# Seven key tiles of a softmax denominator added up on GpSimd and VectorE in float32, with one float32 product in place of seven bf16 ones

## The chip, the cores and the metric

The kernel runs on one core of one Trainium2 chip. The metric is the device time of one execution in microseconds (us). An execution's time is a little longer than the span of its profile.

## The reference

Eight batches of attention with twelve heads, 448 positions and head size 64, on normalised queries and keys, and then a two-layer network on the 3584 x 768 result. Cut to what matters:

```python
q_n = q / (np.linalg.norm(q, axis=-1, keepdims=True) + 1e-06)
k_n = k / (np.linalg.norm(k, axis=-1, keepdims=True) + 1e-06)
scores = np.matmul(q_n, k_n.transpose(0, 1, 3, 2)) / tau
attn = np.exp(scores - np.max(scores, axis=-1, keepdims=True))
attn = attn / (np.sum(attn, axis=-1, keepdims=True) + 1e-09)
x = np.matmul(attn, v)          # heads side by side: (3584, 768)
h = x @ w_in                    # (768, 2048)
out = np.maximum(0.01 * h, h) @ w_out
```

The change is about `np.sum(attn, ...)`, the denominators of the softmax.

## The kernel before

Scores are bounded because queries and keys are normalised, so the kernel takes no maximum. It works with transposed scores: keys lie on the partitions and queries along the free dimension. ScalarE writes exp(scores) as bf16 tiles "pe" of 128 partitions x 896 (line 423). The denominators are then sums over partitions and over seven tiles, which the kernel gets as a product on TensorE with ones (PE in the profile), accumulated in PSUM.

The whole program is in an order written out by hand: each engine carries out its own instructions in the order of the code. Two batches of head pairs go through an older layout (lines 653 to 861). From the third batch on there are 18 *units* of two head pairs each and ten *groups* of one or two units (lines 186 to 191). A unit has seven key tiles (126 in all), and the loop at line 896 goes through them three at a time, in 42 *visits*. A visit does the following.

- `normalise(s)` (line 250): VectorE sums the two parts of the norm, takes the reciprocal, and multiplies queries or keys by it (line 260) into `qn`. `s` is a half of a unit, its queries or its keys; which visit prepares which half is worked out at lines 879 to 882: no half in visits 9, 16, 23, 30 and from 37 on.
- `prepare()` (line 901): VectorE transposes `qn`, and SyncE's DMAs bring it into place; SyncE loads raw data for a later half; GpSimd copies one element of `qn` ("hold", line 619), which makes it wait for VectorE, and then squares the raw data of the half after the next (line 216); VectorE sums the squares of the next half (line 232).
- `quad_tiles` (line 406): PE computes score tiles with eight small matmuls each, ScalarE takes the exponential.
- `group_products(g, e)` (line 427): in the visit after a group's last tile PE makes the denominators (`e` is None: 56 matmuls of pe with ones), in the next one or two visits the products with the values (`e` 0 and 1: 56 matmuls with `vq`). They stand behind the visit's first score tile. `group_logs` and `group_inverse` make 1/denominator on ScalarE by Ln and Exp, and `group_scale` multiplies on VectorE (line 467) into `xT`.
- pieces of the two-layer network of earlier batches (`first`, line 485, and `second`, line 523), dealt out so that PE always has work (lines 930 to 942). `second` ends with a VectorE copy (line 538) into `osb` and a DMA to the output.
- `roots(s + 1)` on ScalarE, before the last of those pieces.

The denominators with ones stand in visits 3, 7, 12, 15, 19, 24, 28, 33 and 38, and for the last group behind visit 41.

The very last `second` copies its 384 columns in two halves, one on VectorE and one on ScalarE, and sends them off with one DMA. In the first microseconds, `load_main` and `load_rem` bring the first pairs in with DMAs from SyncE (SP) and ScalarE's queue (ACT).

Of the kernel before, what the change touches and what calls it, by code (L numbers as in the profile page):

```python
# [8 lines left out]
F32 = mybir.dt.float32  # L9
BF16 = mybir.dt.bfloat16  # L10
AF = mybir.ActivationFunctionType
ALU = mybir.AluOpType
# [4 lines left out]
def kernel(  # L17
# [10 lines left out]
    nc = tc.nc  # L28
    B, H, S, D = q.shape
# [13 lines left out]
    WARM = 20  # L43
    NEWQ = 2 * NQ
    PER = 3
    assert REM == 64 and D == 64

    ctx.enter_context(tc.manual_schedule())
# [4 lines left out]
    qnp = ctx.enter_context(tc.tile_pool(name="qn", bufs=3))  # L53
    ttp = ctx.enter_context(tc.tile_pool(name="tt", bufs=2))
    qtp = ctx.enter_context(tc.tile_pool(name="qt", bufs=6))
    pep = ctx.enter_context(tc.tile_pool(name="pe", bufs=25))
    vqp = ctx.enter_context(tc.tile_pool(name="vq", bufs=2))
    rbp = ctx.enter_context(tc.tile_pool(name="rb", bufs=2))
    xtp = ctx.enter_context(tc.tile_pool(name="xt", bufs=2))
    htp = ctx.enter_context(tc.tile_pool(name="ht", bufs=1))  # L60
    osp = ctx.enter_context(tc.tile_pool(name="os", bufs=3))
# [4 lines left out]
    gp = nc.gpsimd  # L66
# [8 lines left out]
    def banks(count, keep=None):  # L75
        lo, hi = (0, 8) if not deals["apart"] else (0, 4) if count == 2 else (4, 8)
        x = min(
            (i for i in range(lo, hi, count) if not set(range(i, i + count)) & set(kept.values())),
            key=lambda i: max(age[i : i + count]),
        )  # L80
        deals["n"] += 1
        age[x : x + count] = [deals["n"]] * count
        if keep:
            kept[keep] = x
        return ps[:, x] if count == 1 else ps[:, x : x + count]
# [41 lines left out]
    def load_rem(pairs, engs=(nc.sync, nc.sync)):  # L127
        lo, hi = 2 * (pairs[0] % 3), 2 * (pairs[-1] % 3) + 2
        part = early[pairs[0] // 3][:, lo:hi, 3]
        for i, (x, eng) in enumerate(zip((q, k), engs)):  # L130
            eng.dma_start(  # L131
                out=part[64 * i : 64 * i + 64],
                in_=x[0, 2 * pairs[0] : 2 * pairs[-1] + 2, MAIN:S].rearrange("h p d -> p h d"),
            )
# [238 lines left out]
    def totals(j):  # L373
        sm = banks(1)
        strip_products(j, sm, lambda g, ki: ones, lambda g: ones_rem[:, g // 2])
        rb = rbp.tile([128, 2, S], F32, name="rb")[:, 0]
        nc.scalar.activation(rb, sm[:, :S], func=AF.Ln)
        nc.scalar.activation(rb, rb, func=AF.Exp, scale=-1.0)
        rbs[j] = rb
# [21 lines left out]
        if (j, e) in kept:  # L401
            given_back((j, e))

    pq = {}

    def quad_tiles(which):

# [19 lines left out]
    def group_products(g, e):  # L427


        us = [u for u, (gg, _) in enumerate(UNITS) if gg == g]  # L430
        two = len(us) == 2
        po = banks(2)
        for i in range(7):
            for strip in range(4):
                for w in range(2):
                    x, a = strip // 2, strip % 2
                    rows = slice(64 * w, 64 * w + 64)
                    weights = ones[rows] if e is None else (
                        vq[g][rows, strip if two else a, i]
                        .rearrange("p (d e) -> p e d", e=2)[:, e if two else w ^ x]  # L440
                    )
                    nc.tensor.matmul(  # L442
                        out=po[32 * strip : 32 * strip + 32, w, :S],
                        lhsT=weights, rhs=pq[us[x if two else 0], i][rows, a, :],
                        start=(i == 0), stop=(i == 6),
                    )
        return po

    def group_logs(g, po):
        grb[g] = rbp.tile([128, 2, S], F32, name="rb")  # L450
        nc.scalar.activation(grb[g], po[:, :, :S], func=AF.Ln)

    def group_inverse(g):
# [68 lines left out]

    def second(c, ts, half):
        c0, n = chunk_cols(c)
        po2 = banks(1)
        for m in range(MT):
            nc.tensor.matmul(  # L527
                out=po2[:, :HALF],
                lhsT=hT[c][:, m, ts * 128 : (ts + 1) * 128],
                rhs=w_out_sb[:, m, half * HALF : (half + 1) * HALF],  # L530
                start=(m == 0), stop=(m == MT - 1),
            )
        if half == 0:
            osb[c, ts] = osp.tile([128, D_model], F32, name="osb")
        o = osb[c, ts]
        last = c == B - 1 and ts == n // 128 - 1
        cut = HALF // 2 if last and half == 1 else HALF
        nc.vector.tensor_copy(out=o[:, half * HALF : half * HALF + cut], in_=po2[:, :cut])  # L538
        if cut < HALF:
            nc.scalar.copy(out=o[:, half * HALF + cut : (half + 1) * HALF], in_=po2[:, cut:HALF])  # L540
        if half == 1 or last:
            h0 = half * HALF if last else 0
            x, end, row = c0 + ts * 128, c0 + (ts + 1) * 128, 0
            while x < end:
                dst, cnt = rows_of(c, x, end)
                eng = nc.scalar if cut < HALF and row else nc.sync
                eng.dma_start(
                    out=dst[:, h0 : (half + 1) * HALF],
                    in_=o[row : row + cnt, h0 : (half + 1) * HALF],
                )  # L550
                x += cnt
                row += cnt


    work = {}
# [14 lines left out]
    load_main(0, (nc.sync, nc.scalar))  # L570
    load_rem((0,), (nc.sync, nc.scalar))
    load_main(1)
    load_rem((1, 2))
    load_main(2)
    load_main(3)
    load_rem((3, 4, 5))
# [14 lines left out]
    nc.vector.memset(warm, 1.0)  # L591
    ones = cpool.tile([128, 32], BF16, name="ones")
    nc.vector.memset(ones, 1.0)
    ones_rem = cpool.tile([128, 2, 32], BF16, name="ones_rem")
    nc.vector.memset(ones_rem, 0.0)
    for i in range(2):
# [58 lines left out]
    for s in range(NPAIR):  # L655
        j = s // 2 - 1 if s >= 2 else None
        even = s % 2 == 0
        n = s + 2 if 0 < s < NPAIR - 2 else None
        last = s == NPAIR - 1
        if not last:  # L660
            scores(s, (0,))
        if s in (1, 2):
            roots(s + 1)
        scores(s, (1,))
        if j is not None and not even:
            products(j, 1)
        if j is not None and even:
            totals(j)
        elif not last:
            fill(2)  # L670
        if n:
            sums(n, (0,))
        if not last:
            normalise(s + 1)
        if s == 0:
            load_qk(7)
        elif s in (2, 3):
            hold_loads(s + 1)
            load_qk(s + 6)
        if s == 3:  # L680
            sums(n, (1,))
        if late:
            scale(late.pop(), 1)
        if j is not None and not even:
            scale(j, 0)
        if last:
            scale(j, 1)
            sums(NPAIR)
            sums(NPAIR + 1)
            load_w_out(0)  # L690
        else:
            hold(qn[s + 1][:, 6, 0, 0:1])
        squares(s + 3)
        if s == 0:
            load_v_rem(0, range(2, 4))
        if s in (1, 2):
            load_v(s)
        if last:
            load_v(NQ)
            load_v_rem(1)  # L700
        elif s < 2:
            load_w_in(s)
        elif s > 2:
            load_w_in(s - 1)
        if n and even:
            sums(n, (1,))
        scores(s, (2,))
        if last:
            for m in range(2):
                first(0, m, (0, 2))  # L710
            scores(s, (3,))
            for kt in (1, 3):
                for m in range(2):
                    first(0, m, (kt,))
        elif not even:
            fill(2)
            if s == 3:
                roots(n)
                transposes(s + 1)
            scores(s, (3,))  # L720
            if s == 1:
                transposes(s + 1)
                sums(n, (1,))
            fill(2)
        elif s == 0:
            fill(2)
            transposes(1)
            sums(2)
            fill(2)
        else:  # L730
            transposes(s + 1)
            products(j, 0)
            if s == NPAIR - 2:
                scores(s + 1, (0,))
            if n:
                roots(n)
        if j is not None and not even and not last:
            late.append(j)
# [61 lines left out]
    load_v(s // 2 + 2)  # L800
    hold_loads(s + 4)
    load_qk(s + 7)
    squares(s + 6)
    feed_groups(0, 1)

    def settle(s):  # L810
        normalise(s)
        if s >= OLD:
            transposes(s)
        hold(qn[s][:, 6, 0, 0:1])
        squares(s + 2)

    scores(s + 2, (0, 1, 2))
    feed_groups(0, 1)
# [3 lines left out]
    roots(s + 5)  # L822

    scores(s + 3, (0, 1, 2))
    settle(s + 5)
    hold_loads(s + 5)
    load_qk(s + 8)
    feed_groups(0, 1)
# [62 lines left out]
        for n in range(len(visits))  # L891
    ]

    held = []
    fed = 0
    for n, tiles in enumerate(visits):
# [22 lines left out]
        if scaling:  # L919
            prepare()  # L920
        quad_tiles(tiles[1:])
        if g is not None and e is None:
            group_inverse(g)
        for u, i in tiles:
# [15 lines left out]
            now.append(held.pop(0)[1][1])  # L940
            done += w
        fed += done
        for fn in now[:-1]:
            fn()
        roots(s + 1)
        for fn in now[-1:]:
            fn()
    g = len(GROUPS) - 1
    group_logs(g, group_products(g, None))
# [46 lines left out]
```

## Time and profile before

| what | value |
|---|---|
| runs of before | 417.6, 418.37 (median) and 528.36 us |
| the profiled execution | 418.31 us |
| its span | 416.5 us |
| granted TensorE clock | 0.999 |
| the 560 matmuls with ones | 15.1 us busy |
| GpSimd's squares of a half, 36 | 60.9 us busy |

"Busy" is the time in which an engine has an instruction under way; matmuls overlap, so the chain of work that ended last tells better what one of them costs. In the timeline a row is the start, the duration, the engine, the line of the code, the operation, output <- input, shapes and types, and, in brackets, how long the engine had been idle before and what released it. POOL is GpSimd, DVE VectorE, ACT ScalarE, SP SyncE.

### The profile page before, as it was taken

How to read it: one execution, taken by the hardware profiler on the slowest of the kernel's cores; microseconds unless marked ns; L12 is line 12 of the kernel's file. 1: busy time of each engine (PE TensorE's matmuls, PEld its weight loads, DVE VectorE, ACT ScalarE, POOL GpSimd, SP SyncE). 2: the span in 40 equal slices, each digit the busy share in tenths (PEclk: the TensorE clock that was granted, in tenths of full speed). 3: DMA queues.
4: the chain of work that ended last, by engine and by line, in shares of the span. 5: the costliest groups of instructions: out<-in, count | busy, mean ns of one | idle time of the engine just before them, and what ended most of it. 6: DMA issues, size and time to landing. Idle time of an engine off the chain costs nothing.

```text
span 416.5 us, 11298 instructions
## 1 busy us (share of the span) xinstructions
PE 406.0 (97%) x4769; PEld 211.1 (51%) x4785; DVE 221.4 (53%) x386; ACT 250.7 (60%) x432; POOL 114.2 (27%) x149
## 2 busy tenths in 40 slices
PE   8799999999999999999999999999999999999996
PEld 3235555544455555544455555554445555654563
DVE  6778776856678555766484964464621301210021
ACT  4897877288657785667865688547674464014300
POOL 4887343433234132413331433122210000000000
PEclk9999999999999999999999999999999999999999
DMA  7999998684377841884285681742442100020022
GB/s 185 248 219 216 210 234 183 160 237 120 59 209 189 208 115 32 210 229 95 51 190 154 149 232 45 174 126 83 91 90 77 41 39 3 38 77 0 2 76 76
DMA packets 41820, 53.82 MB, mean 129 GB/s; under 512 B 12458, under 2 KB 32170, under 8 KB 41770
## 3 DMA queue, kind: packets, MB, share of 16 engines
q1 hardware_dynamic: 25866, 41.07, 35.1%
q0 software_dynamic: 15488, 11.80, 19.7%
q8 instruction: 37, 0.61, 0.6%
q10 hardware_dynamic: 416, 0.23, 0.2%
q14 instruction: 13, 0.11, 0.1%
HBM read 45.61 MB, written 11.01 MB: 136 GB/s over the span
## 4 chain that ended last, share of the span: by engine, by line
PE 92%; ACT 3%; DVE 2%; DMA 1%; SPq 1%; issue 1%; ACTq 0%; DVEq 0%
PE ps L494 35%; PE ps L527 35%; PE ps L442 9%; PE ps L417 7%; PE ps L366 3%; PE ps L346 2%; ACT pe L355 2%; DVE qn L270 1%; DMA xT<-in_k_dram 1%; PE ps L284 1%; SPq L131 0%; SPq L139 0%; DVE qkT L325 0%; PE ps L608 0%; ACT norms L246 0%
## 5 line engine op out<-in xcount | busy, mean ns | idle before, releaser
L527 PE MATMUL ps<-w_out_sb,hT 128*128 128x384 bf16 x896 | 151.3, 326 | 0.0
L494 PE MATMUL ps<-xT,w_in_sb 128*128 128x384 bf16 (+1 forms) x754 | 150.1, 352 | 0.8 <-issue 0.2
L423 ACT ACTIVATE pe<-ps 128x896 bf16<-128x896 f32 x126 | 108.9, 916 | 46.0 <-PE ps L417 46.0
L527 PEld LDWEIGHTS <-hT 128*128 128x128 bf16 x896 | 85.4, 98 | 64.9 <-issue 10.3
L494 PEld LDWEIGHTS <-w_in_sb 128*128 128x128 bf16 x768 | 72.7, 98 | 74.1 <-issue 9.7
L505 ACT ACTIVATE hT<-ps 128x384 bf16<-128x384 f32 (+1 forms) x128 | 67.5, 553 | 56.0 <-PE ps L494 54.9
L538 DVE COPY osb<-ps 128x384 f32<-128x384 f32 (+1 forms) x56 | 30.9, 551 | 100.4 <-PE ps L527 100.4
L216 POOL TENSOR_TENSOR sq<-qk_h 128x896 f32<-128x896 f32 x36 | 60.9, 1691 | 9.3 <-DMA qk_h<-in_k_dram 6.7
L619 POOL CAST seen<-qn 128x1 f32<-128x1 bf16 x46 | 8.5, 185 | 177.1 <-DVE qn L260 162.5
L260 DVE TENSOR_TENSOR qn<-qk_h,r 128x896 bf16<-128x896 f32 x36 | 43.0, 1195 | 1.2
L355 ACT ACTIVATE pe<-ps 128x896 bf16<-128x896 f32 x42 | 36.1, 917 | 3.3 <-PE ps L346 3.3
L232 DVE TENSOR_REDUCE ss<-sq 128x14 f32<-128x910 f32 x36 | 37.9, 1052 | 0.0
L417 PE MATMUL ps<-qkT 64*32 64x448 bf16 x1008 | 36.5, 353 | 0.0
L253 DVE TENSOR_REDUCE r<-norms 128x14 f32<-128x28 f32 x48 | 8.6, 179 | 49.4 <-ACT norms L246 48.8
L467 DVE TENSOR_TENSOR xT<-ps,rb 128x448 bf16<-128x448 f32 x32 | 18.4, 617 | 23.2 <-PE ps L442 21.5
L306 DVE STREAM_TRANSPOSE tt<-qn 128x448 f32<-128x448 f32 x36 | 29.6, 822 | 0.9
L442 PE MATMUL ps<-pe,vq 64*32 64x448 bf16 x1008 | 27.0, 349 | 0.0
L245 ACT ACTIVATE ss<-ss 128x14 f32<-128x14 f32 x48 | 10.3, 215 | 24.8 <-DVE ss L232 24.0
L417 PEld LDWEIGHTS <-qkT 64*32 64x32 bf16 x1008 | 13.1, 91 | 19.3 <-issue 14.5
L442 PEld LDWEIGHTS <-vq 64*32 64x32 bf16 x1008 | 14.5, 92 | 8.0 <-issue 0.3
L442 PE MATMUL ps<-pe,ones 64*32 64x448 bf16 x560 | 15.1, 349 | 0.0
L346 PE MATMUL ps<-qkT 64*64 64x448 bf16 (+1 forms) x132 | 12.6, 359 | 2.2 <-ACT pe L355 1.3
(54 smaller groups left out, 218.3 us busy)
## 6 DMA issues: line engine op xcount, KB each, us to landing
qk_h<-in_q_dram SPq DMA_DIRECT2D x36, 224.0 KB, 4.0
qk_h<-in_k_dram SPq DMA_DIRECT2D x36, 224.0 KB, 4.6
out_dram<-osb SPq DMA_DIRECT2D x20, 384.0 KB, 2.3
qkT<-tt SPq DMA_DIRECT2D x72, 56.0 KB, 3.3
qkT<-tt SPq DMA_DIRECT2D x36, 112.0 KB, 3.4
vq<-in_v_dram POOLq DMA_DIRECT2D x16, 224.0 KB, 4.9
w_in_sb<-in_moe_w_in_dram POOLq DMA_DIRECT2D x4, 768.0 KB, 10.0
w_out_sb<-in_moe_w_out_dram POOLq DMA_DIRECT2D x2, 1536.0 KB, 21.4
```

The costliest lines, as they stand in the source:

```text
L216: gp.tensor_tensor(sq[:, :, :D], x, x, op=ALU.mult)
L232: nc.vector.tensor_reduce(ss[s], sqs[s], axis=AX.X, op=ALU.add)
L260: nc.vector.tensor_tensor(qn[s].rearrange("p m d e -> p m e d"), raw[s].rearrange(f"p ({t[1:-1]} d) -> p m e d", e=n, d=D), r.rearrange(f" ...
L306: nc.vector.transpose(out=to.rearrange(("p g (c m) -> p m g c", "p g (m c) -> p m g c")[which], m=7), in_=qn[s].bitcast(F32).rearrange("p ...
L355: nc.scalar.activation(out=dst, in_=sc[:, :, :S], func=AF.Exp, scale=inv_tau)
L417: nc.tensor.matmul(out=sc[32 * strip : 32 * strip + 32, a, :S], lhsT=x[rows, c0 : c0 + 32], rhs=x[rows, 0:S], start=True, stop=True,)
L423: nc.scalar.activation(out=pq[u, i], in_=sc[:, :, :S], func=AF.Exp, scale=inv_tau)
L442: nc.tensor.matmul(out=po[32 * strip : 32 * strip + 32, w, :S], lhsT=weights, rhs=pq[us[x if two else 0], i][rows, a, :], start=(i == 0), ...
L494: nc.tensor.matmul(out=pm[:, :n], lhsT=w_in_sb[:, kt, m * 128 : (m + 1) * 128], rhs=xT[c // 2][:, kt, c0 : c0 + n], start=(done + i == 0), ...
L505: nc.scalar.activation(out=hT[c][:, m, :n], in_=pm[:, :n], func=AF.Prelu, alpha=0.01)
L527: nc.tensor.matmul(out=po2[:, :HALF], lhsT=hT[c][:, m, ts * 128 : (ts + 1) * 128], rhs=w_out_sb[:, m, half * HALF : (half + 1) * HALF], st ...
L538: nc.vector.tensor_copy(out=o[:, half * HALF : half * HALF + cut], in_=po2[:, :cut])
```

## The change

From the third batch on, each unit gets an accumulator `acc` (128 x 896, float32; two buffers). GpSimd adds key tiles 1, 2, 4 and 5 to it and VectorE tiles 3 and 6, the first add starting from tile 0. In each visit GpSimd's adds are issued behind the score tiles, VectorE's behind the first piece of the two-layer network. `group_products(g, None)` then makes eight float32 matmuls of ones with `acc` in place of 56 bf16 ones with the tiles. The ones lie in what was the identity matrix. To make room, pe goes from 25 to 23 buffers, and 1/denominator has one buffer in place of two.

```diff
+    ADDS = {i: (nc.vector if i % 3 == 0 else nc.gpsimd) for i in range(1, 7)}
-    pep = ctx.enter_context(tc.tile_pool(name="pe", bufs=25))
+    pep = ctx.enter_context(tc.tile_pool(name="pe", bufs=23))
-    rbp = ctx.enter_context(tc.tile_pool(name="rb", bufs=2))
+    acp = ctx.enter_context(tc.tile_pool(name="acc", bufs=2))
...
-    pq = {}
+    pq, acc, due, summed = {}, {}, [], set()
+
+    def add_up(eng):
+        for u, i in list(due):
+            late = u > 1 and UNITS[u - 2][0] not in summed
+            if ADDS[i] is not eng or late or (i > 1 and u not in acc):
+                continue
+            due.remove((u, i))
+            if i == 1:
+                acc[u] = acp.tile([128, 2, S], F32, name="acc")
+            eng.tensor_tensor(
+                acc[u], pq[u, 0] if i == 1 else acc[u], pq[u, i], op=ALU.add
+            )
...
+        if e is None:
+            for strip in range(4):
+                for w in range(2):
+                    rows = slice(64 * w, 64 * w + 64)
+                    nc.tensor.matmul(
+                        out=po[32 * strip : 32 * strip + 32, w, :S], lhsT=ones_f[rows],
+                        rhs=acc[us[strip // 2 if two else 0]][rows, strip % 2, :],
+                        start=True, stop=True,
+                    )
+            summed.add(g)
+            return po
...
-        grb[g] = rbp.tile([128, 2, S], F32, name="rb")
+        grb[g] = inverse
...
+    ones_f = id128.bitcast(F32)[:, 0:32]
+    nc.vector.memset(ones_f, 1.0)
...
         quad_tiles(tiles[1:])
+        due += [(u, i) for u, i in tiles if i]
+        add_up(gp)
...
-        for fn in now[:-1]:
+        for fn in now[:1]:
+            fn()
+        add_up(nc.vector)
+        for fn in now[1:-1]:
             fn()
         roots(s + 1)
-        for fn in now[-1:]:
+        for fn in now[1:][-1:]:
             fn()
```

The last `second` becomes two pieces of 192 columns, each with its own 16 matmuls, VectorE copy, `osb` tile and DMA from SyncE; ScalarE's copy and DMA there go away:

```diff
-        cut = HALF // 2 if last and half == 1 else HALF
-        nc.vector.tensor_copy(out=o[:, half * HALF : half * HALF + cut], in_=po2[:, :cut])
-        if cut < HALF:
-            nc.scalar.copy(out=o[:, half * HALF + cut : (half + 1) * HALF], in_=po2[:, cut:HALF])
+        pieces = ((0, HALF // 2), (HALF // 2, HALF)) if last and half == 1 else ((0, HALF),)
+        for lo, hi in pieces:
```

In the first microseconds one load moves to the other queue, and the sums and roots of the first pairs are issued at other places; one pair of filler matmuls is dropped. In the stretch between the two layouts one GpSimd squaring (`squares(s + 6)`) moves behind the next `normalise` and hold:

```diff
-    load_rem((1, 2))
+    load_rem((1, 2), (nc.scalar, nc.sync))
...
-        if s in (1, 2):
-            roots(s + 1)
...
-        if n:
+        if n and s > 1:
             sums(n, (0,))
...
+        if s < 2:
+            sums(s + 2, (0, 1) if s == 0 else (0,))
...
-            scores(s, (3,))
             if s == 1:
-                transposes(s + 1)
                 sums(n, (1,))
+                roots(n)
...
         elif s == 0:
-            fill(2)
+            roots(2)
             transposes(1)
-            sums(2)
             fill(2)
...
-    squares(s + 6)
...
-    settle(s + 5)
+    settle(s + 5, (s + 6,))
```

More of the change, by code (lines that the diff above doesn't have):

```diff
@@ L375, in totals @@
         strip_products(j, sm, lambda g, ki: ones, lambda g: ones_rem[:, g // 2])
-        rb = rbp.tile([128, 2, S], F32, name="rb")[:, 0]
+        rb = inverse[:, j % 2]
         nc.scalar.activation(rb, sm[:, :S], func=AF.Ln)
@@ L437, in group_products @@
                     rows = slice(64 * w, 64 * w + 64)
-                    weights = ones[rows] if e is None else (
+                    weights = (
                         vq[g][rows, strip if two else a, i]
@@ L524, in second @@
         c0, n = chunk_cols(c)
[L525 to L535, printed above, removed]
-        last = c == B - 1 and ts == n // 128 - 1
@@ L537, in second @@
-        cut = HALF // 2 if last and half == 1 else HALF
-        nc.vector.tensor_copy(out=o[:, half * HALF : half * HALF + cut], in_=po2[:, :cut])
-        if cut < HALF:
[L540 to L549, printed above, removed]
-                )
-                x += cnt
-                row += cnt
+        last = c == B - 1 and ts == n // 128 - 1
@@ new lines, in second @@
+        pieces = ((0, HALF // 2), (HALF // 2, HALF)) if last and half == 1 else ((0, HALF),)
+        x, end = c0 + ts * 128, c0 + (ts + 1) * 128
+        for lo, hi in pieces:
+            po2 = banks(1)
+            for m in range(MT):
+                nc.tensor.matmul(
+                    out=po2[:, : hi - lo],
+                    lhsT=hT[c][:, m, ts * 128 : (ts + 1) * 128],
+                    rhs=w_out_sb[:, m, half * HALF + lo : half * HALF + hi],
+                    start=(m == 0), stop=(m == MT - 1),
+                )
+            if half == 0 or last:
+                osb[c, ts] = osp.tile([128, D_model], F32, name="osb")
+            o = osb[c, ts]
+            cols = slice(half * HALF + lo, half * HALF + hi)
+            nc.vector.tensor_copy(out=o[:, cols], in_=po2[:, : hi - lo])
+            if half == 1 or last:
+                if not last:
+                    cols = slice(0, D_model)
+                row = 0
+                while row < 128:
+                    dst, cnt = rows_of(c, x + row, end)
+                    nc.sync.dma_start(out=dst[:, cols], in_=o[row : row + cnt, cols])
+                    row += cnt
@@ L593 @@
     nc.vector.memset(ones, 1.0)
+    inverse = cpool.tile([128, 2, S], F32, name="inverse")
     ones_rem = cpool.tile([128, 2, 32], BF16, name="ones_rem")
@@ L718 @@
                 roots(n)
-                transposes(s + 1)
+            transposes(s + 1)
             scores(s, (3,))
             if s == 1:
-                transposes(s + 1)
                 sums(n, (1,))
+                roots(n)
             fill(2)
         elif s == 0:
-            fill(2)
+            roots(2)
             transposes(1)
-            sums(2)
             fill(2)
@@ L802, with settle @@
     load_qk(s + 7)
-    squares(s + 6)
     feed_groups(0, 1)
-    def settle(s):
+    def settle(s, more=()):
         normalise(s)
@@ L814, in settle @@
         hold(qn[s][:, 6, 0, 0:1])
-        squares(s + 2)
+        for x in (*more, s + 2):
+            squares(x)
     scores(s + 2, (0, 1, 2))
```

## The prediction

> **What bounds the kernel now.** I read the page's busy shares first, then the chain of work that ended last, then the groups, and at last the timeline of PE, POOL and DVE through some visits of the third-batch stage (a visit: one turn of the loop at line 896).
>
> ```profile
> span 416.5 us, 11298 instructions
> PE 406.0 (97%) x4769; PEld 211.1 (51%) x4785; DVE 221.4 (53%) x386; ACT 250.7 (60%) x432; POOL 114.2 (27%) x149
> ...
> PE 92%; ACT 3%; DVE 2%; DMA 1%; SPq 1%; issue 1%; ACTq 0%; DVEq 0%
> ...
> L216 POOL TENSOR_TENSOR sq<-qk_h 128x896 f32<-128x896 f32 x36 | 60.9, 1691 | 9.3 <-DMA qk_h<-in_k_dram 6.7
> L260 DVE TENSOR_TENSOR qn<-qk_h,r 128x896 bf16<-128x896 f32 x36 | 43.0, 1195 | 1.2
> ...
> L442 PE MATMUL ps<-pe,ones 64*32 64x448 bf16 x560 | 15.1, 349 | 0.0
> ```
> PE is the limit: 97% busy and 92% of the chain. GpSimd, at 27%, looks free. What PE takes off its list is worth its full time there, as long as PE never waits. The last row is the work that is replaced; the two above it are the nearest rows to the new adds.
>
> ```profile
> 224.89 0.38 PE L417 MATMUL ps<-qkT 64*32 64x448 bf16 x8
> 225.09 1.51 PE L442 MATMUL ps<-pe,ones 64*32 64x448 bf16 x56
> ...
> 239.05 0.76 PE L417 MATMUL ps<-qkT 64*32 64x448 bf16 x24
> ...
> 246.68 0.38 PE L417 MATMUL ps<-qkT 64*32 64x448 bf16 x8
> ```
> Visits 24 to 28 on PE: the first score tile of a visit, and 0.4 us after the visit's start the product with ones. Visits 24, 25 and 26 take 4.72 us each (14.16 to 239.05), visit 27 takes 7.63.
>
> ```profile
> 203.92 1.68 POOL L216 TENSOR_TENSOR sq<-qk_h 128x896 f32<-128x896 f32 x1
> 205.55 1.27 POOL L202 DMA_DIRECT2D vq<-in_v_dram  x2
> 209.78 0.19 POOL L619 CAST seen<-qn 128x1 f32<-128x1 bf16 x1 [2.96 <-DVE qn L260]
> 209.92 1.68 POOL L216 TENSOR_TENSOR sq<-qk_h 128x896 f32<-128x896 f32 x1
> 215.32 0.18 POOL L619 CAST seen<-qn 128x1 f32<-128x1 bf16 x1 [3.73 <-DVE qn L260]
> ```
> ```profile
> 213.54 0.17 DVE L253 TENSOR_REDUCE r<-norms 128x14 f32<-128x28 f32 x1
> 213.75 0.24 DVE L254 RECIPROCAL r<-r 128x14 f32<-128x14 f32 x1
> 214.03 1.17 DVE L260 TENSOR_TENSOR qn<-qk_h,r 128x896 bf16<-128x896 f32 x1
> ```
> These give the steps of a visit that prepares a pair. From the start of VectorE's normalising to its end 1.66 us (213.54 to 215.20); 0.12 to GpSimd's copy of one element ("hold"), which waits for it (215.32); 0.14 to the squares (209.78 to 209.92); 1.63 until GpSimd takes its next instruction (203.92 to 205.55). Together 3.55 us. In before, GpSimd then idles until the next pair.
>
> ```profile
> 62.50 1.68 POOL L216 TENSOR_TENSOR sq<-qk_h 128x896 f32<-128x896 f32 x1 [2.89 <-DMA qk_h<-in_k_dram]
> ```
> ```profile
> 63.35 1.85 DVE L260 TENSOR_TENSOR qn<-qk_h,r 128x896 bf16<-128x896 f32 x1
> ```
> Where the normalising overlaps GpSimd's squares it takes 1.85 in place of 1.17 us: it is done 1.17 after about 64.03, when the squares are nearly over. So such operations of the two engines don't run side by side.
>
> ```profile
> 412.98 0.36 DVE L538 COPY osb<-ps 128x192 f32<-128x192 f32 x1 [2.06 <-PE ps L527]
> 413.37 0.32 ACT L540 COPY osb<-ps 128x192 f32<-128x192 f32 x1 [20.66 <-DVE osb L538]
> ```
> At the end the ACT copy waits for the DVE copy; the output DMA goes out behind both.
>
> **The sum's base.** The profiled execution took 418.31 us (span 416.5 and 1.8 around it); the median of the runs shown is 418.37. I work against 418.31.
>
> **The product.** Removed: 10 products with ones, each 56 matmuls in 1.32 us in the chain, seven waves of eight positions at 0.188 us. Added: 8 float32 products per group; the built program makes each of two weight loads and two matmuls of 448 columns, so 16 matmuls. No row shows a float32 matmul. Bounds from the wave: 0.38 us if the eight positions overlap as now (two waves), 3.0 if none do (16 x 0.188). The order is new: the two matmuls of one product stand directly behind each other at one position, and the next position comes behind them. If PE starts them in order, the second waits for the first and overlaps with the first of the next product: nine steps, 9 x 0.188 = 1.7 us. I take that: 10 x (1.7 - 1.32) = +4 us. The Trainium skill ("FP8 and Floating Point Precision", section Matmul Precision) says that true float32 takes four passes through the array; that would make each step two passes and the group 3.4 us, +20 in place of +4 in the sum. No run yet shows which.
>
> **The adds.** Each of 18 units gets four GpSimd adds (tiles 1, 2, 4, 5) and two VectorE adds (3, 6), 128x896 each. For GpSimd the nearest row is L216, same size and two operands: 1.63 us. Below: a bf16 operand is half the bytes, 1.2. Above: 2.04, the longest L216 (at 56.84). I take 1.63. The Trainium skill ("GPSIMD Engine Reference", Performance versus the Vector engine) gives 4497 ns for an add of 2048 elements, an estimate of 1.97 us for 896; the squares' 1.63 is faster than that, and the sum would be some 18 us higher by it (52 adds in the waits below x 0.34). VectorE: 1.17 by L260, 1.2 with the hand-over.
>
> By share there is room: 72 x 1.63 = 117 us on a GpSimd that is 27% busy. By order there isn't. In after's instruction order the adds of a visit stand behind hold and squares on GpSimd; VectorE's add of tile 3 or 6 waits for the last GpSimd add to the same accumulator, mostly issued in the same visit; the next visit's normalising stands behind that add on VectorE; and the next hold waits for that normalising. So the two engines work in turn: from one normalising to the next 3.55 + 1.63n + 1.2 = 4.75 + 1.63n us with n GpSimd adds: 6.4, 8.0, 9.6 for one, two, three. PE's visits take 4.7 to 7.6. The group's float32 product waits for the add of tile 6, and everything behind it on PE waits too.
>
> I followed this through the stage, visit starts of before shifted by what PE has lost so far. Visits 9, 16, 23 and 30 prepare no pair (VectorE only adds; the lag is made up there), and from 37 on none do. A visit with two GpSimd adds and no VectorE add (0, 7, 14, ...) holds the next hold for 6.7 us.
> - Visit 3: squares of visit 0 end at 86.6, its adds at 89.9; visit 1's normalising ends at 91.1, its VectorE add at 97.4; visit 2's, which overlaps an add, at 103.7. PE wants the sum at 100.4: waits 3.4.
> - Visit 7: 103.7 + 8.0 + 6.4 + 8.0 + 8.0 = 134.1; wanted at 124.04 + 0.4 + 3.8 = 128.2: 6.0.
> - Visit 12: visit 10's normalising starts at 149.2, behind visit 9's add; + 8.0 + 6.4 = 163.6; wanted at 151.50 + 0.4 + 10.2 = 162.1: 1.6.
> - Visit 19: in the same way visit 17's at 196.1, + 14.4 = 210.5; wanted at 194.86 + 0.4 + 12.6 = 207.9: 2.7.
> - Visit 24: the add of visit 23 ends at 241.8; wanted at 224.89 + 0.4 + 15.7 = 241.0: 0.9.
> - Visit 28 (three adds in visit 24, one late): 241.9 + 9.6 + 6.4 + 8.0 + 8.0 = 273.9; wanted at 246.68 + 0.4 + 17.0 = 264.1: 9.9.
> - Visit 33: visit 31's at 295.0, + 14.4 = 309.4; wanted at 279.01 + 0.4 + 27.3 = 306.7: 2.8. The groups at 15 and 38 and the last one have room: the latter has 9.9 us of first-layer products before it.
>
> Waits 27.3 us. If GpSimd's add took 1.2, some 20 less; at 2.04, some 20 more. Score tiles are not late: pairs are prepared three visits ahead. What VectorE's lag holds otherwise is PSUM (copies of line 538 stand behind its adds); PE would then wait for a bank before it waits for the sum, not in addition.
>
> **Buffers.** A two-unit group holds 14 tiles and the nine of three visits until its last product: 23 at most, so 23 buffers fit and cost nothing; one "inverse" in place of two buffers is rewritten a visit after its last reader: nothing, or a wait inside the lag above.
>
> **First us.** PE idles 4.05 us between 10 and 60 us; most that can be won. The q half of the loads for pairs 1 and 2 moves from SP (0.62 us of issue) to ACT's queue, ahead of an ACT that waits for data until 4.11: free, and SP's later loads go 0.62 earlier. Sums of pair 2 move ahead of pair 1's copy on VectorE: two reduces, 0.69 + 0.55, of which 0.4 may delay that copy; roots come later or earlier by about an exponential (0.9). A filler of two matmuls is dropped from idle time: nothing. The squares at 62.50 move behind the hold on GpSimd: the 0.68 lost at 63.35 goes, but PE is busy there. Between -3 and +1; I take -0.5.
>
> **Last us.** 32 matmuls of 192 columns in place of 16 of 384: these took 2.71 us in the chain; half the columns halve a matmul, but a weight load takes 0.098, and 32 of those are 3.1: 0 to +0.4. The ACT copy behind the DVE copy goes (-0.35), and the last DMA carries half the bytes (0 to -1). -0.4.
>
> **Sum:** 418.3 + 4 + 27.3 - 0.5 - 0.4 = 448.7, say 449 us.
>
> **The rivals.**
> *GpSimd's add is cheap and the waits vanish; faster.* The bf16 operand speaks for it; against it, squares of 384 to 896 elements cost 1.66 ns an element (0.82 and 1.68). At 1.0 us the waits are still about 8 us (visits 7 and 28), which two-wave products (-9.4) pay back; it ends ahead only below that. At 0.7: 418.3 - 9.4 + 3 - 0.9 = 411.
> *The float32 products run one behind another.* 3.0 us each group: 13 more, 462. For it: the same position twice in a row; against it: the eight-fold overlap in L442. The four passes of the page named above, in order, would give 466.
> *Half of it.* The adds take about 1.1 and the products 0.8 to 1.3: waits of 5 to 12 us, savings up to 5: 413 to 426.
>
> **How the numbers follow.** Forecast 0.53 (449, own range 430 to 468: the add at 1.2 to 2.0), serial products 0.20 (455 to 485), half of it 0.17 (within 2%), cheap adds 0.10 (404 to 414, 0.07 of it below 410). A measurement of this kernel tells about 2% from no change, 410 to 427 us here. Faster 0.07, same 0.17 + 0.03 = 0.20, slower 0.53 + 0.20 = 0.73. The range 412 to 470 leaves out most of the cheap case and the upper half of the serial one.
>
> **What would show it.** PE's wait for the sums on DVE, longest at the groups of visits 7 and 28, some 27 us in all, or PE waiting for DVE copies just before; GpSimd's adds near 1.63; VectorE's adds waiting for POOL; products of a group near 1.7 us; POOL busy near 230 us. I am wrong if PE stays without waits, if the adds take about 1 us, or if the group's product is far from 1.7.

## The result and the profile after

The changed kernel takes 471.4 us (median; 470.1 to 472.3), the kernel before 418.2 on the same chips: ratio 1.127, with a 95% interval of 1.125 to 1.129. It is slower by 53 us; the forecast was 449, its range ended at 470. One execution of the kernel before took 528.36 us and is left out of the ratio.

The page of the changed kernel, its share lines, its chain of work that ended last, and the groups of the adds and the new product (busy time and mean ns, then the idle time before them and its releaser):

```profile
span 470.5 us, 10724 instructions
...
PE 424.0 (90%) x4399; PEld 213.3 (45%) x4399; DVE 264.5 (56%) x424; ACT 250.3 (53%) x431; POOL 249.6 (53%) x221
...
PE 32%; POOL 30%; issue 19%; DMA 8%; DVE 6%; ACT 3%; SPq 1%; POOLq 0%
...
L415 POOL TENSOR_TENSOR acc<-acc,pe 128x896 f32<-128x896 f32 x54 | 101.7, 1884 | 5.8 <-DVE acc L415 2.6
...
L415 DVE TENSOR_TENSOR acc<-acc,pe 128x896 f32<-128x896 f32 x36 | 41.1, 1141 | 87.0 <-POOL acc L415 87.0
...
L450 PE MATMUL ps<-acc,id 64*32 64x448 f32 x160 | 17.6, 645 | 16.2 <-DVE acc L415 14.2
```

No engine is full any more: GpSimd and VectorE are a little over half busy and PE has fallen from 97 to 90%. The chain says why. It was 92% PE; now PE and GpSimd have a third each, and 19% is time in which nothing shown was being waited for. VectorE stood idle for 87.0 us in front of its 36 adds, always for GpSimd. The span grew by 54.0 us: PE's idle time by 36.0 (46.5 against 10.5), its busy time by 18.0, though it has fewer matmuls (4399 recorded against 4769).

What PE waited for, in the waits of the changed kernel (us in all, times, longest):

```profile
PE ps L450 <- DVE acc L415: 14.2, 5, 4.5
PE ps L430 <- DVE xT L491: 10.7, 7, 4.2
PE ps L555 <- DVE osb L565: 5.7, 4, 2.2
PE ps L430 <- DVE osb L565: 2.9, 2, 2.5
PE ps L450 <- DVE r L254: 2.0, 1, 2.0
PE ps L430 <- DVE xT L497: 1.8, 2, 0.9
```

The rows of L450 are the waits for a sum, 16.2 us (the one of 2.0 is put down to the VectorE instruction behind the add). The rows of L430 and L555 are score tiles and second-layer matmuls that need a PSUM bank which VectorE has not yet emptied: 21.1 us, more than the sums.

One turn of the two engines, and PE behind it, from the timeline:

```profile
287.17 1.68 POOL L217 TENSOR_TENSOR sq<-qk_h 128x896 f32<-128x896 f32 x1
...
288.81 3.83 POOL L415 TENSOR_TENSOR acc<-acc,pe 128x896 f32<-128x896 f32 x2
...
292.67 1.09 DVE L415 TENSOR_TENSOR acc<-acc,pe 128x896 f32<-128x896 f32 x1 [4.05 <-POOL acc L415]
...
293.82 0.97 PE L450 MATMUL ps<-acc,id 64*32 64x448 f32 x4 [4.53 <-DVE acc L415]
...
294.17 1.16 DVE L261 TENSOR_TENSOR qn<-qk_h,r 128x896 bf16<-128x896 f32 x1
...
295.39 0.18 POOL L641 CAST seen<-qn 128x1 f32<-128x1 bf16 x1 [2.75 <-DVE qn L261]
295.53 1.68 POOL L217 TENSOR_TENSOR sq<-qk_h 128x896 f32<-128x896 f32 x1
```

Squares, two GpSimd adds, VectorE's add, normalising, hold, squares again: 8.36 us (287.17 to 295.53), in which each of the two engines idles for most of the time that the other adds.

And how a bank gets late, in visit 9, which prepares no pair:

```profile
150.04 1.87 POOL L415 TENSOR_TENSOR acc<-pe 128x896 f32<-128x896 bf16 x1
150.11 2.75 DVE L415 TENSOR_TENSOR acc<-acc,pe 128x896 f32<-128x896 f32 x1 [2.71 <-POOL acc L415]
...
152.78 1.14 DVE L491 TENSOR_TENSOR xT<-ps,inverse 128x448 bf16<-128x448 f32 x2
153.45 0.35 PE L430 MATMUL ps<-qkT 64*32 64x448 bf16 x1 [2.40 <-DVE xT L491]
```

VectorE waits 2.71 us for GpSimd's adds; then its own add takes 2.75 us in place of 1.09, since GpSimd's next add started 0.07 us ahead of it; the multiplication that empties a bank (L491) stands behind both, and PE stops for it. The group's product with ones began only 14 us later, at 167.47.

### The profile page after: what moved, and what is told of

Its sections match the earlier page's. It is cut to its first block, busy times and chain, and to the rows that moved or that the text cites. A ratio compares the mean times of both kernels' runs of the same rounds, so it can differ in the third digit from the quotient of the medians.

```text
span 470.5 us, 10724 instructions
## 1 busy us (share of the span) xinstructions
PE 424.0 (90%) x4399; PEld 213.3 (45%) x4399; DVE 264.5 (56%) x424; ACT 250.3 (53%) x431; POOL 249.6 (53%) x221
## 4 chain that ended last, share of the span: by engine, by line
PE 32%; POOL 30%; issue 19%; DMA 8%; DVE 6%; ACT 3%; SPq 1%; POOLq 0%
POOL acc L415 21%; PE ps L555 14%; PE ps L518 12%; POOL sq L217 5%; DMA w_out_sb<-in_moe_w_out_dram 5%; DVE acc L415 2%; DMA qk_h<-in_k_dram 2%; PE ps L466 2%; PE ps L430 2%; DVE qn L261 1%; POOL vq L203 1%; PE ps L450 1%; PE ps L367 1%; DMA xT<-in_q_dram 1%; ACT pe L356 1%
## 5 line engine op out<-in xcount | busy, mean ns | idle before, releaser
L555 PE MATMUL ps<-w_out_sb,hT 128*128 128x384 bf16 (+1 forms) x912 | 157.6, 332 | 7.3 <-DVE osb L565 5.7
L555 PEld LDWEIGHTS <-hT 128*128 128x128 bf16 x912 | 88.5, 100 | 75.6 <-issue 22.8
L415 POOL TENSOR_TENSOR acc<-acc,pe 128x896 f32<-128x896 f32 x54 | 101.7, 1884 | 5.8 <-DVE acc L415 2.6
L415 DVE TENSOR_TENSOR acc<-acc,pe 128x896 f32<-128x896 f32 x36 | 41.1, 1141 | 87.0 <-POOL acc L415 87.0
L430 PE MATMUL ps<-qkT 64*32 64x448 bf16 x1008 | 46.8, 375 | 15.4 <-DVE xT L491 10.7
L261 DVE TENSOR_TENSOR qn<-qk_h,r 128x896 bf16<-128x896 f32 x36 | 49.1, 1363 | 1.2
L415 POOL TENSOR_TENSOR acc<-pe 128x896 f32<-128x896 bf16 x18 | 34.7, 1928 | 18.0 <-ACT pe L436 11.0
L430 PEld LDWEIGHTS <-qkT 64*32 64x32 bf16 x1008 | 16.4, 94 | 43.1 <-issue 39.9
L450 PE MATMUL ps<-acc,id 64*32 64x448 f32 x160 | 17.6, 645 | 16.2 <-DVE acc L415 14.2
L491 DVE TENSOR_TENSOR xT<-ps,inverse 128x448 bf16<-128x448 f32 x32 | 18.3, 613 | 11.9 <-PE ps L466 11.7
```

Source lines behind the costliest of these rows:

```text
L261: nc.vector.tensor_tensor(qn[s].rearrange("p m d e -> p m e d"), raw[s].rearrange(f"p ({t[1:-1]} d) -> p m e d", e=n, d=D), r.rearrange(f" ...
L415: eng.tensor_tensor(acc[u], pq[u, 0] if i == 1 else acc[u], pq[u, i], op=ALU.add)
L430: nc.tensor.matmul(out=sc[32 * strip : 32 * strip + 32, a, :S], lhsT=x[rows, c0 : c0 + 32], rhs=x[rows, 0:S], start=True, stop=True,)
L555: nc.tensor.matmul(out=po2[:, : hi - lo], lhsT=hT[c][:, m, ts * 128 : (ts + 1) * 128], rhs=w_out_sb[:, m, half * HALF + lo : half * HALF + ...
```

## The experiments

All medians are of runs beside the kernel before on the same chips (417.9 to 418.3).

**Only the ends and the buffers.** The adds go, the old product with ones stays; 23 buffers, one inverse, head and tail as in the change.

```diff
-        due += [(u, i) for u, i in tiles if i]
-        add_up(gp)
...
-        add_up(nc.vector)
```

> The changed kernel without the adds and with the product of ones as it was: what is left are the first and last us, the single 1/denominator buffer and 23 pe buffers. If the loss of the change lies in the adds alone, this ends 1 to 2 us ahead of before (the two traces show the third-batch stage starting 0.9 us earlier and the end 0.6 us shorter): 416 to 417.5 us. If the buffers or the moved first us carry part of the loss: above 420.

417.3 us, ratio 0.9985 (0.9973 to 0.9996). The ends bring 0.8 us between the medians; the whole loss is in the adds and their product.

**Without the hold.** GpSimd's copy of one element, which makes it wait for VectorE's normalising, is dropped in the visits.

```diff
-                hold(qn[s][:, 6, 0, 0:1])
                 squares(s + 2)
```

> The changed kernel without GpSimd's copy of one element (hold) in the visits of the third-batch stage, so that the squares no longer wait for VectorE's normalising; all adds stay. Turn-taking (squares, GpSimd adds, VectorE add, next normalising, hold, squares): the circle is cut, a visit costs GpSimd 1.63 + 2 x 1.83 = 5.3 us beside PE's 5.9, the waits fall to about 10 us: 418 to 432 us. Rival, the operations of both engines exclude each other and their sum is the bound (15.1 us a unit beside 13.8 on PE): 440 us or more.

464.2 us (1.108 to 1.113): 7 us won of 53. My expectation failed; the time is in the rival's range, 440 or more. That doesn't show the rival's mechanism, since VectorE's adds still continue GpSimd's accumulator here: the kernel with the same adds apart, below, takes 436.7. VectorE still waits 40.9 us for GpSimd's adds, and where the hold no longer keeps the two apart they collide:

```profile
261.87 1.68 POOL L217 TENSOR_TENSOR sq<-qk_h 128x896 f32<-128x896 f32 x1
261.95 2.55 DVE L415 TENSOR_TENSOR acc<-acc,pe 128x896 f32<-128x896 f32 x1 [3.03 <-POOL acc L415]
```

The add that takes 1.09 us alone takes 2.55 when GpSimd's squares start 0.08 us ahead: it ends 0.95 us after they do. That agrees with the Trainium skill ("SBUF — State Buffer", section SBUF: two separate sides), by which a VectorE operation with two SBUF inputs and a GpSimd operation that reads SBUF take turns on one pair of ports, the whole instruction at a time. The normalising (L261) rose to 1973 ns in the mean, from 1363.

**The sums made, but not used.** Is it PE's wait for the sum? All adds stay; the denominators come from the old product, so that PE never waits for a sum.

```diff
         if e is None:
-            for strip in range(4):
-                for w in range(2):
...
             summed.add(g)
-            return po
```

> The changed kernel with all adds made and not used: the denominators come from the 56 matmuls with ones as before, so PE never waits for a sum, and GpSimd's and VectorE's order is unchanged. If only the wait for the sum costs: 416 to 425 us. If the late VectorE itself holds PE, because PSUM banks are given back behind its adds: most of the loss stays, 445 to 465 us.

467.1 us (1.114 to 1.120), 2 us above the range that I gave for late banks. PE needs no sum and the time hardly falls. In its waits:

```profile
DVE acc L415 <- POOL acc L415: 87.6, 27, 4.8
...
PE ps L430 <- DVE osb L556: 13.2, 5, 4.2
...
PE ps L430 <- DVE xT L482: 8.7, 7, 3.6
```

VectorE waits for GpSimd as long as before, and PE's long waits are now all for the banks that VectorE empties (copies of `osb`, multiplications into `xT`).

**The same adds, apart.** As the last kernel, but VectorE's adds go into a tile of their own.

```diff
+            if eng is nc.vector:
+                own = scp.tile([128, 2, S], F32, name="own")
+                eng.tensor_tensor(own, pq[u, i - 1], pq[u, i], op=ALU.add)
+                continue
```

> As adds_unused (all adds made, denominators by the old product with ones), but VectorE's two adds per unit no longer continue GpSimd's accumulator: they add tile 2 to 3 and tile 5 to 6 into a tile of their own. Same number of adds on each engine, same places in the order; only VectorE's wait for GpSimd's accumulator is gone. Theory of the dependence (VectorE, waiting for GpSimd's adds, holds up its own later copies and the normalising, and those hold up PE and GpSimd): what is left is GpSimd's load as in gp4_b16, which lost some 15 us against its sum: 425 to 436. Rival (the load, the contention of the two engines, does it): 455 to 470, as adds_unused with 467.

436.7 us (1.041 to 1.046), 0.7 us above what the dependence theory gave (425 to 436) and 18 us below the rival's range. The number of adds on each engine is that of the last kernel. VectorE and GpSimd are even busier (263.7 and 251.6 us there), while VectorE's wait in front of its adds has gone from 87.6 us to 2.3:

```profile
PE 411.8 (95%) x4783; PEld 214.8 (49%) x4799; DVE 298.4 (69%) x424; ACT 249.8 (57%) x431; POOL 280.7 (65%) x221
...
L418 DVE TENSOR_TENSOR own<-pe 128x896 f32<-128x896 bf16 x36 | 59.3, 1648 | 2.3 <-ACT pe L441 2.2
```

The adds themselves got longer: VectorE's 1648 ns in the mean against 1122, GpSimd's to its accumulator 2375 against 1901.

So of the loss 30 us (467.1 to 436.7) come from the shared accumulator: VectorE, with the emptying of PE's banks queued behind, waits for GpSimd's adds. (The edit also frees GpSimd from waiting for VectorE's adds, which was 1.3 us.) The slower matmuls behind PE's waits are in these 30 us: the granted clock was 0.966 there and is 0.992 here. The adds as such cost 19 us (417.3 to 436.7).

**GpSimd alone, four adds.** It adds tiles 0 to 4, the last add in bf16, and the product with ones takes three waves (sum, tiles 5 and 6).

```diff
+        order = range(7) if e is not None else [*range(LAST + 1, 7), LAST]
...
-        due += [(u, i) for u, i in tiles if i]
+        due += [(u, i) for u, i in tiles if 0 < i <= LAST]
```

> GpSimd alone adds up tiles 0 to 4 (four adds, the last one rounds to bf16), VectorE adds nothing, and PE takes the sum and tiles 5 and 6 in three bf16 waves (0.57 us a group in place of 1.32). Turn-taking: without an add on VectorE's queue nothing holds the normalising, GpSimd has 11.5 us of work in a unit's 13.8; no waits of note: 418.2 - 7.5 - 1.5 = 409 us, up to 414 with some waits for the fourth add. Rival, GpSimd's adds hold up VectorE's operations with two SBUF operands enough to reach PE: 425 us or more.

425.8 us (1.018 to 1.022); I expected 409 to 414, and the rival's 425 or more was met. Without VectorE's adds, and with this product, 46 of the 53 us are back, but GpSimd's four a unit still run late in two places, one of which this shows:

```profile
128.13 0.37 PE L455 MATMUL ps<-a,ones 64*32 64x448 bf16 x4 [3.90 <-POOL a L416]
```

That is the group of visit 7; the other wait is at visit 28, 5.34 us, the two that the prediction named as the longest. These 9.2 us are over half of the 17 us by which the kernel misses the 409 of its sum; the cause of the rest is open.

**GpSimd alone, three adds and two.** `LAST = 3` and `LAST = 2`.

> GpSimd alone adds tiles 1, 2 and 3 to tile 0 (54 adds; the last one of a unit rounds to bf16) and the product with ones takes this sum and tiles 4 to 6 in bf16: four waves of eight in place of seven. VectorE adds nothing. My theory (the loss comes from VectorE's adds standing between the two engines and from GpSimd's lag; with gp4_b16 there were two waits of 3.9 and 5.3 us left behind GpSimd's fourth add): with a quarter of the adds gone the two waits mostly vanish. 418.1 - 10 x 3 x 0.188 (waves) - 0.7 (both ends) = 411.8, plus up to 2 us of waits: 411 to 414. Rival (any GpSimd add beside VectorE's normalising delays VectorE by 0.8 us and with it the score tiles or the PSUM banks): 54 adds lose more than they save, 418 to 424.

> As gp3_b16 with tiles 1 and 2 alone (36 adds on GpSimd), five waves of eight. My theory: nothing waits; 418.1 - 10 x 2 x 0.188 - 0.7 = 413.6, so 413 to 415. Rival (each add beside the normalising costs): 416 to 420. Against gp3_b16 it tells whether a GpSimd add costs something by itself: by my theory gp3_b16 is 0 to 2 us lower, by the rival gp2_b16 is.

413.7 us (0.987 to 0.990) and 414.0 us (0.988 to 0.991). Two adds come out as the sum gives (413.6) with no PE wait for an add in the trace. Three are 1.9 us above theirs (411.8), and with overlapping intervals no better than two; where the 1.9 us go is open.

**The same two adds on VectorE.**

```diff
-        add_up(gp)
...
         for fn in now[:1]:
             fn()
+        add_up(nc.vector)
```

> The same two adds as in gp2_b16, and so the same product, on VectorE: 36 VectorE adds, as many as in the changed kernel, issued at the same place, but they wait only for ScalarE's tiles, not for GpSimd. Tells the load on VectorE from the dependence. My theory (the dependence on GpSimd's adds is what costs): the adds are 36 x 1.1 = 40 us of VectorE that lies idle 47% of the time; 413 to 416, as gp2_b16. Rival (VectorE's adds by themselves stand ahead of the normalising and of the PSUM copies and so hold up PE): 420 to 440.

416.2 us (0.994 to 0.997), just above my range of 413 to 416. 36 adds on VectorE at the place where the changed kernel has its 36 cost 2.2 us against the same on GpSimd; the rival's 420 to 440 is out. VectorE's load by itself isn't what costs the 53 us.

**Two adds on each engine, apart and in a chain.** Both with bf16 sums and three waves: GpSimd adds tiles 0, 1, 2 and VectorE 3, 4, 5 into a second sum; or VectorE adds tiles 3 and 4 to GpSimd's sum.

```diff
+            c = 0 if i < 3 else 3
+            fresh = (u, c) not in acc
+            if fresh:
...
+            eng.tensor_tensor(acc[u, c], pq[u, i - 1] if fresh else acc[u, c], pq[u, i], op=ALU.add)
```

> GpSimd adds tiles 0, 1 and 2, VectorE tiles 3, 4 and 5, each into a bf16 sum of its own; the product with ones takes both sums and tile 6: three waves in place of seven. 36 adds on each engine, none waits for the other engine. My theory: nothing waits, 418.2 - 10 x 4 x 0.188 - 0.7 = 410.0; with ve2_b16's loss of 2 us beside VectorE's adds up to 412: 409 to 412. Rival (load on both engines at once costs): 415 to 425.

> As indep22 with the same 36 adds on each engine and three waves, but in one chain: GpSimd adds tiles 1 and 2 to tile 0, VectorE then adds tiles 3 and 4 to that sum. Dependence theory: worse than indep22 by the turn-taking, with half of the changed kernel's GpSimd adds: some 4 to 15 us, 414 to 425. Rival (the dependence as such costs nothing, only the load counts): within 1 us of indep22.

417.8 us (0.9987 to 1.0004) and 419.2 us (1.001 to 1.004). Both miss: the first was to be 409 to 412 and lies in its rival's range (the load on both engines at once costs: 415 to 425). The chain costs only 1.4 us here, not 4 to 15. With half of GpSimd's adds VectorE waits for them for 25.6 us in all in place of 87.0. The first has PE idle for 15.6 us, 5 more than the kernel with GpSimd's two alone (10.6), mostly in short waits for ScalarE's exponentials and VectorE's copies. Here two engines adding side by side lose more than the two waves are worth.

**Matmuls of no use in the waits.** The changed kernel with 16 extra matmuls ahead of the sums of visits 7, 28 and 33.

```diff
+        if n in (7, 28, 33):
+            wm = banks(1)
+            for i in range(16):
+                nc.tensor.matmul(
...
```

> The changed kernel with 16 matmuls 128x512 (some 3.4 us) of no use, put ahead of the denominators in visits 7, 28 and 33, where PE waited for a sum (2.92, 4.53 and 2.60 us). They fill the waits and leave the rest as it is. Theory that the lower granted clock behind a wait (0.58 in the 8 us after the wait at 272.67 us, 0.74 after 293.82) is a part of the loss by itself: the clock comes out above 0.963 and the time 2 to 9 us under 471.4, in spite of 10 us of added work. Rival (the clock falls for another reason, or slow matmuls only fill time in which PE would wait for VectorE anyway): the time stays at 471 or rises to 476, even if the clock rises.

467.7 us (1.116 to 1.120) against 471.4 (1.125 to 1.129): 3.7 us faster with 10 us of work added, mean clock of the profiled executions 0.970 against 0.963. The stretch behind the wait at 293.8 us shows it (columns: stretch, its length, busy time and instructions of each engine, then the granted clock). The changed kernel:

```profile
294.00:304.00 10.00, 10.00 (x64) 4.68 (x52) 3.18 (x4) 6.00 (x10) 5.58 (x4) 0.74 0.24 64
```

With the filler:

```profile
294.00:304.00 10.00, 10.00 (x147) 5.39 (x132) 5.02 (x8) 7.54 (x15) 5.87 (x6) 1.00 0.24 63
```

From 288 to 294 us PE is busy for 1.47 us in the one and for 5.00 in the other, and the sum lands 0.1 us apart. Behind it comes the same work in both. PE is busy throughout, but at a clock of 0.74 against 1.00: the 42 first-layer matmuls take 8.43 us (from 296.22) against 7.00 (from 294.99), and the next visit starts at 304.58 against 301.92. (The counts of 64 and 147 don't compare: the second stretch reaches into the next visit's many small matmuls.) So this wait costs PE its length and some 2.6 us behind it.

**A version that beats both.** GpSimd alone, with two adds a unit in the groups of visits 7 and 28, four in the last two groups, three in the rest.

```diff
-    LAST = 3
+    LAST = (3, 2, 3, 3, 3, 3, 2, 3, 4, 4)
```

> As gp3_b16, GpSimd alone, but with two adds a unit in the groups whose sums PE waited for in gp4_b16 (visits 7 and 28), four in the last two groups, where GpSimd has little else, and three in the others: 30 waves fewer, as in gp3_b16, which was 1.9 us above its sum of 411.8. Theory (those 1.9 us are waits behind GpSimd's adds in the crowded stretches): 411.5 to 412.5. Rival (a GpSimd add beside VectorE's normalising costs wherever it stands): 413 to 414, as gp3_b16.

412.4 us, ratio 0.9869 (0.9852 to 0.9885), as the theory had it. It is the fastest here, 5.4 us below the kernel before; its interval overlaps that of three adds everywhere. PE is 98% busy and waits for no add.

## Why the prediction was right or wrong

The direction was right, and so was the turn-taking of the two engines; where it stops PE was wrong in large part. The price was too low by 22 us, and by 32 but for the product, which was priced 9.7 us too high: that the forecast came this near is partly luck. Point by point:

- **PE's waits, 27.3 us: this step failed.** Its sentence was that a wait for a PSUM bank comes "before it waits for the sum, not in addition". The waits are 16.2 us for sums and 21.1 for banks, mostly in other visits than the sums', and with the sums not used at all the kernel still takes 467.1. I followed the circle and let PE run at the old pace between the product visits. But every copy that empties a bank stands in the same queue as VectorE's adds, so the circle can stop PE in any visit. The starts of the product visits show it:

| visit | before, us | after, us | lag | predicted lag |
|---|---|---|---|---|
| 3 | 100.02 | 99.18 | -0.8 | 0 |
| 7 | 124.04 | 131.42 | 7.4 | 3.8 |
| 12 | 151.50 | 167.27 | 15.8 | 10.2 |
| 19 | 194.86 | 221.03 | 26.2 | 12.6 |
| 24 | 224.89 | 259.54 | 34.7 | 15.7 |
| 28 | 246.68 | 288.17 | 41.5 | 17.0 |
| 33 | 279.01 | 329.93 | 50.9 | 27.3 |

  The lag grows by 1.7 us a visit in the mean, in steps. In the eight visits of the products from 3 to 33 it grew by 24.5 us in all, less than I had given them (27.3 us of waits and 0.4 a product). In the other 23 from visit 3 to 33 it grew by 31.6, where I had put nothing: visits 9, 16, 23 and 30, in which I had it made up, alone brought 2.9, 4.5, 2.0 and 0.6. From visit 3 to 38 a visit took 6.16 us before (100.02 to 315.49) and 7.76 after (99.18 to 370.82). My own circle, 4.75 + 1.63n us at 72/42 = 1.71 adds a visit, gives 7.54; with the add as measured 7.97, less where no pair is prepared. Multiplying that by the visits would have come nearer than the waits counted one by one. The prediction also gave PE's visits as 4.7 to 7.6 us; visits 12, 28 and 33 took 8.62, 8.94 and 9.89 in the kernel before.
- **GpSimd's add, 1.63 us: mis-sized.** It took 1884 ns, 1928 from two bf16 tiles. By 0.25 us a piece, with some 52 adds in the waits, that is 13 us by the prediction's own working. The Trainium skill ("GPSIMD Engine Reference", Performance versus the Vector engine) led to an estimate of 1.97 us, nearer than the row I preferred, a tensor multiplied by itself; whether it is the second tensor that makes the add longer, no run shows.
- **The clock: missing from the sum.** The longest wait of PE in before was 1.7 us, at a clock of 0.999. PE's busy time rose by 18.0 us although the new product is cheaper; an estimate from the mean clock, 0.036 of 470.5 us, gives 17. The filler won back 3.7 net. The share of the slow clock in the 53 us was not measured by itself.
- **The product, +4 us: wrong in the other direction.** The rows of the changed kernel:

```profile
259.74 0.94 PE L450 MATMUL ps<-acc,id 64*32 64x448 f32 x16
260.49 0.56 PE L430 MATMUL ps<-qkT 64*32 64x448 bf16 x16
```

  The sixteen matmuls hold PE for 0.75 us (259.74 to 260.49) where nothing waits: two waves of eight at 0.375, twice the 0.188 of a bf16 wave. A group saves 0.57 us, 5.7 in all. The eight positions do overlap; "the second waits for the first" was wrong. The rate agrees with the four passes of the Trainium skill ("FP8 and Floating Point Precision", Matmul Precision): two matmuls at double time. That they would come in order was my addition to it, and the 3.4 us that I worked out by it are out.
- **VectorE's add, 1.17 to 1.2 us:** 1.09 alone, 2.55 to 2.75 where GpSimd was just ahead. I had used the taking of turns for the normalising (63.35 us) but not for the add.
- **First and last us, -0.9:** -0.8 in the kernel with these and the buffers alone. Right.
- **The rivals:** cheap adds and the half of it are out by the add's 1.88 us, serial products by the 0.75 us. What came was none of them: the forecast's own turn-taking, stopping PE in more places.

By the four kernels that change one thing after the other: ends and buffers -0.8 us, the adds on two engines that don't wait for each other +19, VectorE's wait for GpSimd's accumulator +30, and using the sums +4 (467.1 to 471.4), in which, by the 0.57 us a group, 5.7 are saved by the cheaper product and so 10 lost by waiting for the sums (an estimate). That the parts would be the same in another order isn't shown.

## What to carry to other kernels

Before work is moved to an engine that is 27% busy, ask what stands behind it in the queues, and avoid making a busy engine's helper wait for it: here 72 adds on GpSimd and 36 on VectorE lost 53 us, and 54 on GpSimd alone, with nobody else in the chain, won 5. When two engines take turns, price the whole stage by the length of a turn times the number of turns, not by the waits at the points where the result is wanted; here that gives 7.54 us a visit against 7.76 measured. Leave a tensor in bf16 parts that PE can add for 0.188 us a wave rather than add it all elsewhere.

## What the runs showed that I had not expected

- The granted TensorE clock falls behind some waits of PE of two microseconds and more. In the changed kernel, behind a wait of 4.18 us:

```profile
272.67 1.10 PE L430 MATMUL ps<-qkT 64*32 64x448 bf16 x8 [4.18 <-DVE xT L491]
273.22 3.16 PE L466 MATMUL ps<-pe,vq 64*32 64x448 bf16 x56
```

  These take 0.38 and 1.51 us in other visits; the clock was 0.50 from 272.6 to 276 us, 0.58 from 272 to 280, and 1.00 again from 280 on. The Trainium skill ("TensorE: Matmul & The Clock Gate", section Part 1: The HAM clock gate) says that PE runs at half rate after an idle window of about 3.4 us that runs freely, until it has been busy for another. The half rate agrees. Shorter waits were not all alike: behind 2.21 us at 127.32 sixteen second-layer matmuls took 4.17 us in place of 2.77, behind 1.84 us at 256.85 they took 2.76, and behind the 2.40 us at 153.45 the clock was 1.00. A window that runs freely would fit that; that 2.21 us can be enough is less than that window.
- A bf16 operand does not make GpSimd's add cheaper: 1879 ns from bf16 to bf16 (the kernel with two separate sums), 1884 with a float32 accumulator. VectorE's does get cheaper: 658 ns in the mean in the chain with bf16 throughout, 1141 in the changed kernel.
